# Bias of the first pair straight from the running sums, constants placed behind these, and output tiles copied in halves by two engines

## The chip, the core and the metric

The kernel runs on one core of a Trainium2 chip. The core has five engines with queues of their own: TensorE (PE: matmuls and transposes), VectorE (DVE), ScalarE (ACT), GpSimd (POOL), and SyncE (SP), which issues most of the DMAs; ScalarE issues some. Each engine takes its instructions in a fixed order and waits on semaphores for what others produce. The metric is the device time of one execution in microseconds.

## The reference

Causal attention over 4 batches of 8 heads, 576 positions and 64 columns a head, with a bias from running sums of `s`; the heads side by side are 2304 tokens of 512 columns, and two MLPs of width 2048 follow.

```
scores = q @ k.T / 8
cum    = cumsum(max(s, 0))
scores = where(causal, -1e9, scores + min(-(cum[:, None] - cum[None, :]), 0))
x      = softmax(scores) @ v
h      = relu(x @ w_in);  x = (h * h) @ w_out
h      = x @ w2_in;       out = max(0.01 * h, h) @ w2_out
```

## The kernel before

All matmuls are made from high and low halves of float32 values (three passes, `PASSES`), so each operand is split: ScalarE copies the high half, another engine subtracts it to get the low half.

**Attention** (to about 370 us) goes over 16 pairs of heads; two heads share the 128 partitions. `load_qk` brings q and k (for the first pair alone with `i=0`: k by ScalarE's queue, q by SP's; for the second with `i=1`; then for two pairs at a time). `turn` (L252) transposes k and q on VectorE into a tile of tag `yt`, copies the high half on ScalarE and subtracts on GpSimd. The tag `yt` has two buffers, and so have most others that matter here one to four: a tile that takes a buffer must wait until whoever used it is done. Here `running_sums` (L179) uses both buffers of `yt` first, for `one` and `neg`, and `turn` of the first pair takes them next.

The bias enters the scores as a fourth matmul over four rows a head: `ag` holds, for the queries and the keys, rows of the running sum `ka` (high and low), of ones and of minus ones. `running_sums` clamps `s`, scans it, makes `ka` on VectorE, and writes all four kinds of rows for all heads to the DRAM scratch `aug`; `load_bias` (L246) reads a pair's rows back into `ag`, which GpSimd cleared before.

For each pair, `STEPS` gives seven steps of scores (kinds 0, 2, 3 and 4 for the two heads): `scores` on TensorE, `maxima` on VectorE with the mask (L315), `exponentials` on ScalarE (L339), two steps later `flip` (transposes on TensorE, L349, and copies out), then `values`, `gather`, `spread` and `scale`. Kind 4 is the last 64 rows of both heads at once (L289). Two banks of tag `S` hold scores; the next scores wait until the maxima have read them. Between these, weights are converted one by one by `weight` (L98 to L112): first step on ScalarE (L103, L106) and VectorE (L104, L105), then GpSimd (L108) and VectorE (L109, L111). The staging tile `wst` has one buffer in this stage, so the DMA of a weight goes out when L109 of the one before is done. Matmuls of the first MLP layer (`up1`) fill TensorE's gaps.

**The MLPs** follow: the rest of `up1`, `down1`, and from about 645 us `layer2`, over blocks of 512 tokens (the last of 256). In `layer2` each of 16 chunks `fc` gives hidden values `g`, and `down` adds a chunk to one accumulator bank for each 128 tokens; the last two chunks of a block are added at its end, then ScalarE copies each bank to a tile `o` and SP issues its DMA to the output.

**Order.** A scheduler with a timeline of its own sets the order in which each engine's queue is filled; `after(i)` puts instructions of the same engine as `i` behind `i` and says nothing of other engines. So a change in one place can move instructions elsewhere. DMAs take turns on eight semaphores: a DMA is issued only when the one that used its semaphore before has landed.

## Time and profile before

| | |
|---|---|
| median of 3 runs | 1044.83 us (1044.23 to 1047.97) |
| the profiled execution | 1046.09 us, of it the span 1044.3 us |
| TensorE busy | 1002.3 us, 96% of the span |
| VectorE busy | 558.3 us, 53% |
| ScalarE busy | 519.5 us, 50% |
| GpSimd busy | 226.1 us, 22% |
| chain that ended last | TensorE 56%, DMA 4%, VectorE 2% |

The profile is one execution. An engine's busy share over the whole span says little about a single stage: the same engine can be what all others wait for in one stretch and be free in the next. A row of a timeline gives the start, the duration, the engine, the line and the operation with its tiles (out<-in); a row may hold several instructions that follow each other (xcount), and in brackets stands the idle time of the engine before it and what ended it. PEclk is TensorE's granted clock as a share of the full one.

### The profile page before, as it was taken

How to read it: one execution, taken by the hardware profiler on the slowest of the kernel's cores; microseconds unless marked ns; L12 is line 12 of the kernel's file. 1: busy time of each engine (PE TensorE's matmuls, PEld its weight loads, DVE VectorE, ACT ScalarE, POOL GpSimd, SP SyncE). 2: the span in 40 equal slices, each digit the busy share in tenths (PEclk: the TensorE clock that was granted, in tenths of full speed). 3: DMA queues.
4: the chain of work that ended last, by engine and by line, in shares of the span. 5: the costliest groups of instructions: out<-in, count | busy, mean ns of one | idle time of the engine just before them, and what ended most of it. 6: DMA issues, size and time to landing. Idle time of an engine off the chain costs nothing.

```text
span 1044.3 us, 15068 instructions
## 1 busy us (share of the span) xinstructions
PE 1002.3 (96%) x5312; PEld 834.2 (80%) x5312; DVE 558.3 (53%) x1262; ACT 519.5 (50%) x1126; POOL 226.1 (22%) x294
## 2 busy tenths in 40 slices
PE   4878989899999999999999999999999999999998
PEld 3666867778888878898788889888888888888897
DVE  5778878873586524777875448753222322322322
ACT  4667878886787656754443334533312322322232
POOL 6455546631232002223221112210000000000000
PEclk9999999899999999999999999999999999999999
DMA  7546465453532155866775447401100200100010
GB/s 140 116 119 131 115 181 128 137 117 110 126 93 94 53 173 187 267 192 199 235 227 174 132 143 226 133 24 37 44 1 1 81 1 1 61 1 1 1 41 21
DMA packets 152476, 111.30 MB, mean 107 GB/s; under 512 B 98992, under 2 KB 121008, under 8 KB 152400
## 3 DMA queue, kind: packets, MB, share of 16 engines
q1 hardware_dynamic: 139072, 91.01, 31.6%
q10 hardware_dynamic: 13328, 19.32, 5.2%
q8 instruction: 42, 0.69, 0.3%
q14 instruction: 34, 0.28, 0.1%
HBM read 76.69 MB, written 33.62 MB: 106 GB/s over the span
## 4 chain that ended last, share of the span: by engine, by line
PE 56%; DMA 4%; DVE 2%; issue 1%; ACT 1%; POOL 0%; ACTq 0%; SPq 0%; DVEq 0%; POOLq 0%
PE tr L682 19%; PE h L692 9%; PE S L692 9%; PE h L477 6%; PE tr L657 6%; PE S L657 3%; PE h L657 3%; DMA wst<-in_moe_w_in_dram 2%; DMA wst<-in_moe_w_out_dram 1%; DVE wt L109 1%; DMA gl<-gscr 1%; ACT wt L103 0%; DMA xh<-xscr 0%; DVE gh L442 0%; DMA xscr<-xo 0%
## 5 line engine op out<-in xcount | busy, mean ns | idle before, releaser
L477 PE MATMUL h<-xs,w 128*128 128x512 f32 (+1 forms) x960 | 228.0, 382 | 2.9 <-DVE w L111 1.3
L477 PEld LDWEIGHTS h<-xs,w 128*128 128x128 f32 x960 | 162.7, 191 | 33.0 <-DVE w L111 2.1
L682 PE MATMUL tr<-wo,g 128*128 128x512 f32 x756 | 180.9, 389 | 0.0
L682 PEld LDWEIGHTS tr<-wo,g 128*128 128x128 f32 x756 | 141.1, 188 | 28.8
L108 POOL TENSOR_TENSOR wt<-wt,wst 128x512 uint32<-128x512 uint32 x64 | 90.1, 1408 | 287.7 <-DVE wt L105 232.2
L698 DVE TENSOR_TENSOR r<-S,r 128x512 f32<-128x512 f32 (+1 forms) x40 | 25.5, 637 | 170.1 <-ACT r L697 170.1
L657 PE MATMUL tr<-gh,wo 128*128 128x512 f32 (+1 forms) x576 | 111.9, 354 | 0.0
L692 PE MATMUL S<-xs,w 128*128 128x512 f32 (+1 forms) x480 | 106.9, 368 | 1.1 <-ACT xs L441 1.1
L692 PE MATMUL h<-xs,w 128*128 128x512 f32 (+1 forms) x480 | 107.3, 368 | 0.0
L657 PEld LDWEIGHTS tr<-gh,wo 128*128 128x128 f32 x576 | 94.8, 189 | 14.6
L339 ACT ACTIVATE t<-t,m 128x128 f32<-128x128 f32 (+2 forms) x144 | 83.2, 580 | 35.5 <-DVE m L315 35.0
L692 PEld LDWEIGHTS S<-xs,w 128*128 128x128 f32 x480 | 84.8, 188 | 16.9 <-ACT xs L441 1.6
L692 PEld LDWEIGHTS h<-xs,w 128*128 128x128 f32 x480 | 84.9, 188 | 15.7
L697 ACT ACTIVATE r<-S 128x512 f32<-128x512 f32 (+1 forms) x40 | 22.2, 555 | 147.5 <-PE S L692 147.4
L315 DVE CUSTOM_DVE_ANT_0 t<-S,mask 128x128 f32<-128x128 f32 (+2 forms) x144 | 64.7, 480 | 46.4 <-PE S L299 20.9
L442 DVE TENSOR_TENSOR gh<-gl,gh 128x512 fp32r<-128x512 f32 (+1 forms) x80 | 62.2, 780 | 48.0 <-ACT gh L441 47.5
L441 ACT ACTIVATE gh<-gl 128x512 fp32r<-128x512 f32 (+1 forms) x80 | 46.2, 586 | 76.6 <-PE h L657 36.3
L349 PE MATMUL tr<-ident,t 128*128 128x128 f32 x384 | 69.1, 290 | 10.0 <-ACT t L339 8.8
L442 DVE TENSOR_TENSOR g<-r,g 128x512 fp32r<-128x512 f32 (+1 forms) x80 | 50.9, 644 | 38.5 <-ACT g L441 36.6
L441 ACT ACTIVATE g<-r 128x512 fp32r<-128x512 f32 (+1 forms) x80 | 46.6, 589 | 43.5 <-DVE r L698 43.5
L103 ACT ACTIVATE wt<-wst 128x512 f32<-128x512 f32 x64 | 42.5, 664 | 50.8 <-DMA wst<-in_moe_w_in_dram 35.8
L349 PEld LDWEIGHTS tr<-ident,t 128*128 128x128 f32 x384 | 46.5, 145 | 25.8 <-ACT t L339 13.7
(105 smaller groups left out, 1450.3 us busy)
## 6 DMA issues: line engine op xcount, KB each, us to landing
wst<-in_moe_w_in_dram SPq DMA_DIRECT2D x32, 512.0 KB, 4.0
gscr<-gs ACTq DMA_DIRECT2D x32, 512.0 KB, 4.4
wst<-in_moe_w_out_dram SPq DMA_DIRECT2D x32, 512.0 KB, 3.9
gl<-gscr SPq DMA_DIRECT2D x64, 256.0 KB, 2.8
xscr<-xo SPq DMA_DIRECT2D x32, 144.0 KB, 2.5
out_dram<-o SPq DMA_DIRECT2D x18, 256.0 KB, 2.4
xh<-xscr SPq DMA_DIRECT2D x16, 256.0 KB, 2.8
zscr<-ys SPq DMA_DIRECT2D x16, 256.0 KB, 3.5
```

What stands on the lines that cost most here:

```text
L103: nc.scalar.activation(f32(t), f32(hw), AF.Abs)
L108: nc.gpsimd.tensor_tensor(t, t, lw, ALU.add)
L315: return nc.vector.tensor_tensor_reduce(t[:, a:z], sc, msk, -QK_SCALE, first, ALU.add, ALU.min, m).ins
L339: done = nc.scalar.activation(t[:, a:z], t[:, a:z], AF.Exp, bias=m[:, c:c + 1], scale=-1.0, accum_out=sums[:, s0:s0 + 1])
L349: nc.tensor.transpose(tr[:, c * P:(c + 1) * P], t[:, c * P:(c + 1) * P], ident)
L441: a = nc.scalar.activation(out[0], x, AF.Copy)
L442: b = nc.vector.tensor_tensor(out[1], x, f32(out[0]), ALU.subtract)
L477: nc.tensor.matmul(h[:, :w], win[0, fc][:, a, c * P:(c + 1) * P], xs[j, c][:, z, :w], start=(c == 0 and y == 0), stop=(c == KC - 1 and y = ...
L657: nc.tensor.matmul(y[e][:, :w], wout[0, fc][:, a, e * P:(e + 1) * P], gh[:, z, :w], start=(fc == 0 and x == 0), stop=(fc == FC - 1 and x = ...
L682: nc.tensor.matmul(acc[i], g[:, a, i * P:(i + 1) * P], wout[1, fc][:, z], start=(fc == 0 and x == 0), stop=(fc == FC - 1 and x == 2))
L692: nc.tensor.matmul(h[:, :w], win[1, fc][:, a, c * P:(c + 1) * P], xs[c][:, z, :w], start=(c == 0 and x == 0), stop=(c == KC - 1 and x == 2))
L698: nc.vector.tensor_tensor(r[:, :w], h[:, :w], r[:, :w], ALU.max)
```

## The change

Four things are changed.

1. **First pair's bias.** `running_sums` gets the first pair's `ag` and issues six small DMAs into it straight from `ka` and `neg` (four of one row for both heads, by SP and ScalarE in turn, and two from `neg`). The constant rows of `ag` (ones on the query side, zeros on the key side) are written by ScalarE beforehand. The four DMAs to `aug` are issued behind these, all by SP; `load_bias` does nothing for the first pair.
2. **Constants and memsets.** The memsets of `ident`, `mask` and `mask4` are written together ahead of the loads, and GpSimd's selects and memsets stand under `after(raw["sums"])`, the scan.
3. **First pair's low halves** of q and k are subtracted by VectorE, no longer by GpSimd.
4. **End of a block in `layer2`.** `down` is written tile by tile, and each tile `o` is copied in two halves of 256 columns, by ScalarE and VectorE, and sent by two DMAs, by SP and ScalarE.

```diff
@@ -167,16 +167,13 @@
             before[i.engine] = i
 
     def constants():
-        nc.vector.memset(ident, 0.0)
         nc.gpsimd.affine_select(ident, ident, [[-1, P]], ALU.not_equal, 1.0, 0, 1)
-        nc.vector.memset(mask, 0.0)
         nc.gpsimd.affine_select(mask[:, S - P:], mask[:, S - P:], [[-1, P]], ALU.is_ge, -1.0e9 / QK_SCALE, 0, 1)
-        nc.vector.memset(mask4, 0.0)
         for p0 in (0, 64):
             nc.gpsimd.affine_select(mask4[p0:p0 + 64, S // 2 - 64:], mask4[p0:p0 + 64, S // 2 - 64:], [[-1, 64]],
                                     ALU.is_ge, -1.0e9 / QK_SCALE, 0, 1)
 
-    def running_sums(at):
+    def running_sums(at, ag):
 
         sp, cum = [at.tile([BH, S], F32, tag="t", name="t", bufs=TB) for _ in range(2)]
         one, neg = [at.tile([BH, S], F32, tag="yt", name="yt", bufs=2) for _ in range(2)]
@@ -186,13 +183,21 @@
         nc.gpsimd.memset(neg, -1.0)
         yield
         nc.vector.tensor_scalar(sp, sp, 0.0, 1.0 / QK_SCALE, ALU.max, ALU.mult)
-        nc.vector.tensor_tensor_scan(cum, one, sp, 0.0, ALU.mult, ALU.add)
+        raw["sums"] = nc.vector.tensor_tensor_scan(cum, one, sp, 0.0, ALU.mult, ALU.add).ins
         nc.vector.tensor_copy(ka[:, 0], cum)
         nc.vector.tensor_tensor(ka[:, 1], cum, f32(ka[:, 0]), ALU.subtract)
-        nc.sync.dma_start(aug[:, 0:2, 0], one.unsqueeze(1).to_broadcast([BH, 2, S]))
-        nc.sync.dma_start(aug[:, 2:4, 1], neg.unsqueeze(1).to_broadcast([BH, 2, S]))
-        nc.sync.dma_start(aug[:, 0:2, 1], f32(ka))
-        nc.scalar.dma_start(aug[:, 2:4, 0], f32(ka))
+        h0, h1 = pairs[0].h
+        for z in range(2):
+            nc.sync.dma_start(f32(ag[z:z + 65:64, 1]), f32(ka[h0:h1 + 1:h1 - h0, z]))
+            nc.scalar.dma_start(f32(ag[2 + z:z + 67:64, 0]), f32(ka[h0:h1 + 1:h1 - h0, z]))
+        for e in range(2):
+            raw["sent"] = nc.sync.dma_start(f32(ag[64 * e + 2:64 * e + 4, 1]), neg[0:2]).ins
+        yield
+        with after(raw["sent"]):
+            nc.sync.dma_start(aug[:, 0:2, 1], f32(ka))
+            nc.sync.dma_start(aug[:, 2:4, 0], f32(ka))
+            nc.sync.dma_start(aug[:, 0:2, 0], one.unsqueeze(1).to_broadcast([BH, 2, S]))
+            nc.sync.dma_start(aug[:, 2:4, 1], neg.unsqueeze(1).to_broadcast([BH, 2, S]))
 
     class Pair:
 
@@ -246,6 +251,8 @@
     def load_bias(x):
         p = pairs[x]
         p.ag, p.last = ags[x % 2]
+        if x == 0:
+            return
         for e in range(2):
             nc.sync.dma_start(f32(p.ag[64 * e:64 * e + 4]), aug[p.b * H + p.h[e]])
 
@@ -259,7 +266,7 @@
         yt = at.tile([P, S], F32, tag="yt", name="yt", bufs=2)
         nc.vector.transpose(yt, raw[which][:, p.i])
         nc.scalar.activation(hi, yt, AF.Copy)
-        nc.gpsimd.tensor_tensor(lo, yt, f32(hi), ALU.subtract)
+        (nc.vector if x == 0 else nc.gpsimd).tensor_tensor(lo, yt, f32(hi), ALU.subtract)
 
     def turn_v(at, x, e):
         p = pairs[x]
@@ -497,24 +504,30 @@
         for x in range(2):
             ags.append((at.tile([P, 2, S], F32R, tag=f"ag{x}", name=f"ag{x}"),
                         at.tile([P, 3, P], F32R, tag=f"la{x}", name=f"last{x}")))
-        sums = running_sums(at)
+        warm = at.tile([P, 64], F32, tag="warm", name="warm")[:, 0:1]
+        for t in (warm, ident, mask, mask4):
+            nc.vector.memset(t, 0.0)
+        sums = running_sums(at, ags[0][0])
         next(sums)
         load_qk(at, 0, 0)
-        warm = at.tile([P, 64], F32, tag="warm", name="warm")[:, 0:1]
-        nc.vector.memset(warm, 0.0)
         with after(raw["issued"]):
             nc.scalar.activation(warm, warm, AF.Exp)
-        constants()
-        for t in ags[0]:
-            nc.gpsimd.memset(f32(t), 0.0)
-        next(sums, None)
+        nothing = warm.to_broadcast([P, S])
+        for z in range(2):
+            nc.scalar.activation(ags[0][0][:, z], nothing, AF.Copy, scale=0.0, bias=1.0 - z)
+        next(sums)
+        with after(raw["sums"]):
+            constants()
         turn(at, 0, "k")
         turn(at, 0, "q")
+        next(sums, None)
         load_bias(0)
         load_qk(at, 0, 1)
         load_v(at, 0)
-        for t in ags[1]:
-            nc.gpsimd.memset(f32(t), 0.0)
+        with after(raw["sums"]):
+            nc.gpsimd.memset(f32(ags[1][0]), 0.0)
+            for x in range(2):
+                nc.gpsimd.memset(f32(ags[x][1]), 0.0)
         scores(0, 0)
 
         for x in range(len(pairs)):
@@ -676,8 +689,8 @@
             xs.append(t)
         acc = [bank("tr") for _ in range(w // P)]
 
-        def down(fc, g):
-            for i in range(w // P):
+        def down(i, *chunks):
+            for fc, g in chunks:
                 for x, (a, z) in enumerate(PASSES):
                     nc.tensor.matmul(acc[i], g[:, a, i * P:(i + 1) * P], wout[1, fc][:, z],
                                      start=(fc == 0 and x == 0), stop=(fc == FC - 1 and x == 2))
@@ -700,13 +713,17 @@
             tick(*done)
             prev.append((fc, g))
             if len(prev) > DEPTH:
-                down(*prev.pop(0))
-        for x in prev:
-            down(*x)
+                chunk = prev.pop(0)
+                for i in range(w // P):
+                    down(i, chunk)
         for i in range(w // P):
+            down(i, *prev)
             o = lo.tile([P, DM], F32, tag="yf", name="o", bufs=OB)
-            nc.scalar.activation(o, acc[i], AF.Copy)
-            nc.sync.dma_start(out[n + i * P:n + (i + 1) * P, :], o)
+            rows, half = slice(n + i * P, n + (i + 1) * P), DM // 2
+            nc.scalar.activation(o[:, :half], acc[i][:, :half], AF.Copy)
+            nc.vector.tensor_copy(o[:, half:], acc[i][:, half:])
+            nc.sync.dma_start(out[rows, :half], o[:, :half])
+            nc.scalar.dma_start(out[rows, half:], o[:, half:])
 
     late = ctx.enter_context(ExitStack())
     with tc.tile_pool(name="mg", bufs=1) as mg, tc.tile_pool(name="mx", bufs=1) as mx:
```

How instructions stand in the queues, at three places. First SyncE's queue from the start of the program on (`t` is `s`, `yt` is `one` or `neg`), before:

```order
L184 DMA t<-in_s_dram 32x576
L226 DMA qr<-in_q_dram 32x18x32 x4
L192 DMA aug<-yt 32x2x576
L193 DMA aug<-yt 32x2x576
L194 DMA aug<-ka 32x2x576
L226 DMA kr<-in_k_dram 32x18x32 x3
L250 DMA ag_83<-aug 4x1152 x2
L226 DMA kr<-in_k_dram 32x18x32
```

and with the change:

```order
L181 DMA t<-in_s_dram 32x576
L231 DMA qr<-in_q_dram 32x18x32 x4
L231 DMA kr<-in_k_dram 32x18x32 x3
L191 DMA ag_83<-ka 2x576 x2
L194 DMA ag_83<-yt 2x576 x2
L197 DMA aug<-ka 32x2x576
L198 DMA aug<-ka 32x2x576
L199 DMA aug<-yt 32x2x576
L200 DMA aug<-yt 32x2x576
L231 DMA kr<-in_k_dram 32x18x32
```

The reads of `one` and `neg` (`aug<-yt`) have moved from ahead of the sums to behind them and behind six other DMAs, and three loads of k for the second pair have moved ahead of the sums.

Second, GpSimd's queue at the start, with what each instruction waits for, before:

```order
L186 MEMSET yt 32x576
L171 ISA
L171 AFFINE_SELECT ident<-ident 128x128 [waits DVE_49]
L509 MEMSET ag_83 128x1152
L509 MEMSET last_84 128x384
L241 MEMSET vp 64x128
L517 MEMSET ag_85 128x1152
L517 MEMSET last_86 128x384
```

and with the change:

```order
L183 MEMSET yt 32x576
L170 ISA
L170 AFFINE_SELECT ident<-ident 128x128 [waits DVE_49]
L246 MEMSET vp 64x128
L528 MEMSET ag_85 128x1152
L530 MEMSET last_84 128x384
L530 MEMSET last_86 128x384
L246 MEMSET vr 64x128
```

One of the two long memsets is gone; the others wait for nothing, as before, and the select waits for VectorE's count, which the memset of `ident` raises.

Third, ScalarE's queue at the end of the third pair and the start of the fourth (L339 and L346 are the exponentials, L103 and L106 the first step of a weight, L593 and L606, L400 and L407 copies out of TensorE's banks), before:

```order
L400 ACTIVATE xo<-tr 64x320 x2
L593 ACTIVATE pT_686<-tr 128x3x128
L339 ACTIVATE t,sums<-t,m 128x512
L103 ACTIVATE wt<-wst 128x512
L106 ACTIVATE wst<-wst 128x512
L400 ACTIVATE xo<-tr 64x256
L339 ACTIVATE t,sums<-t,m 128x512
L400 ACTIVATE xo<-tr 64x256
L593 ACTIVATE pT_686<-tr 128x4x128
L339 ACTIVATE t,sums<-t,m 128x576
L339 ACTIVATE t,sums<-t,m 128x128
L339 ACTIVATE t,sums<-t,m 128x256
```

and with the change:

```order
L407 ACTIVATE xo<-tr 64x320 x2
L103 ACTIVATE wt<-wst 128x512
L106 ACTIVATE wst<-wst 128x512
L346 ACTIVATE t,sums<-t,m 128x512
L606 ACTIVATE pT_691<-tr 128x3x128
L407 ACTIVATE xo<-tr 64x256
L346 ACTIVATE t,sums<-t,m 128x512
L407 ACTIVATE xo<-tr 64x256
L606 ACTIVATE pT_691<-tr 128x4x128
L346 ACTIVATE t,sums<-t,m 128x576
L346 ACTIVATE t,sums<-t,m 128x128
L103 ACTIVATE wt<-wst 128x512
```

Both weights' first steps have moved up, the one ahead of an exponential of 512 columns, the other (before, three exponentials further down) ahead of the last three exponentials of a step; on VectorE, L104 has moved up likewise, ahead of a copy and a maximum, and on TensorE the eight matmuls of the last rows (L289) have moved behind four transposes and two matmuls of the values.

## Rows read from the trace of the kernel before

**Rows 1.** Busy time by stretch: stretch, length, busy time of each engine (instructions), PEclk, DMA.

```profile
660.00:1040.00 380.00, 380.00 (x1767) 318.14 (x1765) 123.36 (x204) 110.97 (x199) 8.84 (x6) 1.00 0.08 26
```

**Rows 2.** Timeline of VectorE at the start: start, duration, engine, line, operation.

```profile
2.90 2.07 DVE L188 TENSOR_SCALAR t<-t 32x576 f32<-32x576 f32 x1 [1.40 <-DMA t<-in_s_dram]
5.07 1.35 DVE L189 TENSOR_TENSOR_SCAN t<-yt,t 32x576 f32<-32x576 f32 x1
6.45 0.45 DVE L190 CAST ka<-t 32x576 fp32r<-32x576 f32 x1
6.94 0.75 DVE L191 TENSOR_TENSOR ka<-t,ka 32x576 fp32r<-32x576 f32 x1
7.61 0.76 DVE L260 STREAM_TRANSPOSE yt<-kr 128x576 f32<-128x576 f32 x1
```

**Rows 3.** Timeline of GpSimd at the start.

```profile
2.10 1.05 POOL L509 MEMSET ag<- 128x1152 f32 x1
...
4.60 0.72 POOL L517 MEMSET last<- 128x384 f32 x1
...
9.24 2.75 POOL L262 TENSOR_TENSOR Y<-yt,Y 128x576 fp32r<-128x576 f32 x2 [1.45 <-ACT Y L261]
```

**Rows 4.** Timeline of all engines up to the first scores.

```profile
8.40 1.34 ACT L261 ACTIVATE Y<-yt 128x576 fp32r<-128x576 f32 x2 [4.07 <-DVE yt L260]
...
10.60 0.62 SPq L250 DMA_DIRECT2D ag<-aug  x2
...
12.05 0.69 PE L299 MATMUL S<-Y 64*128 64x128 f32 x4 [1.77 <-POOL Y L262]
...
12.71 0.81 PE L299 MATMUL S<-ag 64*128 64x128 f32 x2
```

**Rows 5.** DMA issues from 0 to 20 us: queue, count, size, us to landing.

```profile
aug<-ka SPq DMA_DIRECT2D x1, 144.0 KB, 2.1
```

**Rows 6.** Timelines of ScalarE, VectorE and TensorE at the third and fourth pairs.

```profile
53.62 0.72 ACT L339 ACTIVATE t<-t,m 128x512 f32<-128x512 f32 x1
55.77 0.66 ACT L103 ACTIVATE wt<-wst 128x512 f32<-128x512 f32 x1 [1.35 <-DMA wst<-in_moe_w_in_dram]
57.16 0.71 ACT L339 ACTIVATE t<-t,m 128x512 f32<-128x512 f32 x1
63.77 0.68 ACT L103 ACTIVATE wt<-wst 128x512 f32<-128x512 f32 x1 [0.95 <-DMA wst<-in_moe_w_in_dram]
64.92 1.24 ACT L261 ACTIVATE Y<-yt 128x576 fp32r<-128x576 f32 x2
56.47 0.43 DVE L104 TENSOR_SCALAR wt<-wt 128x512 f32<-128x512 f32 x1 [2.01 <-ACT wt L103]
59.32 0.68 DVE L109 SCALAR_TENSOR_TENSOR wt<-wst,wt 128x512 uint32<-128x512 uint32 x1
53.80 0.66 PE L289 MATMUL S<-Y,last 128*128 128x288 f32 x3
58.01 0.66 PE L349 MATMUL tr<-ident,t 128*128 128x128 f32 x4 [1.79 <-ACT t L339]
58.81 0.55 PE L299 MATMUL S<-Y 64*128 64x128 f32 x6
73.94 0.84 PE L289 MATMUL S<-Y,last 128*128 128x288 f32 x3 [2.68 <-DVE m L315]
```

**Rows 7.** Busy time by stretch, as in group 1.

```profile
72.00:76.00 4.00, 2.06 (x10) 2.05 (x11) 2.90 (x9) 1.78 (x5) 2.80 (x6) 0.78 0.52 153
```

**Rows 8.** Timelines of ScalarE and SyncE at the end.

```profile
1036.10 0.38 ACT L697 ACTIVATE r<-h 128x256 f32<-128x256 f32 x1 [1.14 <-PE h L692]
1039.98 1.09 ACT L708 ACTIVATE o<-tr 128x512 f32<-128x512 f32 x2 [2.59 <-PE tr L682]
1040.60 0.82 SPq L709 DMA_DIRECT2D out_dram<-o  x2
```

**Rows 9.** VectorE's instructions by line and shape: count, busy us, mean ns.

```profile
L662 DVE COPY ys<-tr 128x256 f32<-128x256 f32 x2 | 0.8, 408 | 0.0
```

## The prediction

> **What bounds the kernel now.** I read the busy table by stretches first. From 660 to 1040 us TensorE is busy without a gap [rows 1], so nothing that happens beside it there can move the time, and the change leaves TensorE's order there alone. Time can be won or lost only before the first scores, in the attention stage while TensorE still waits for other engines, and after the last matmul.
>
> Next I read the start engine by engine. VectorE's clamp of `s` begins when `s` has landed, at 2.90, and takes 2.07 us, while a cast of the same 576 columns takes 0.45; the reader is to see GpSimd's long memsets over the same microseconds [rows 2, 3]. Scan, cast, subtraction and the transposes follow each other without a gap [rows 2]. ScalarE makes the high halves, GpSimd the low ones (2.75 for both), and TensorE's third matmul starts at 12.05, released by GpSimd; the bias, which went out to DRAM and came back, is there at 12.71 [rows 3, 4]. So two chains end within 0.7 us: the low halves on GpSimd, and the bias by way of `aug`. To gain, the change has to shorten both.
>
> Then the third and fourth head pairs (44 to 80 us), because the order of the changed kernel differs there. ScalarE converts a weight tile in its first step (L103) when its DMA has landed, and waits for that at 55.77 and at 63.77; VectorE's L104 waits for L103 at 56.47; TensorE stands 1.79 us at 58.01 and 2.68 us at 73.94 [rows 6]. Whatever stands behind L103 or L104 on its engine waits for the weight too.
>
> Last, the end: two copies from 1039.98 on and two DMA issues from 1040.60 [rows 8].
>
> **The change part by part.** *Memsets and constants.* The masks' memsets on VectorE move a line, to the same place: nothing. The `after(raw["sums"])` names an instruction of VectorE, and what stands under it runs on GpSimd; in the order of the changed kernel GpSimd's selects wait for the memsets only and its memsets for nothing, so they are not behind the sums in time. What does change is that `ag` of the first pair (1.05 us) leaves GpSimd for ScalarE, which is idle then. From 2.1 on GpSimd still has one memset of 1152 columns (1.05), two of 384 (a third of that each) and two small ones of some 0.2: to about 4.15. The clamp starts at 2.90 again. Before, it ended at 4.97, that is, it got through when the second long memset ended near 4.6, and the `last` memset that started there took 0.72 [rows 2, 3]. If it gets through at the end of the one long memset that is left (3.3), it ends at 3.75; if only after the last memset, at 4.6. I take the middle, 4.2: 0.8 us gained, with 0.4 to 1.2 as ends.
>
> The Trainium skill (SBUF — State Buffer, section Who interferes with whom) calls the port pair that VectorE and GpSimd share an exclusive lock, held for one whole instruction. By that the clamp would follow the memset that is running and end at 3.75, and the sum would be 0.45 us lower; the row of before speaks against it, since there GpSimd began three more memsets while the clamp waited [rows 2, 3].
>
> *Bias without the round trip.* From 4.2: scan 1.35, cast 0.45, subtraction 0.75 and gaps of 0.05 give the cast at 6.1 and the subtraction at 6.9 [rows 2]. The six small DMAs into `ag` go out between 6.1 and 7.8 on SP and ScalarE and land 2.1 us after their issue (the landing of `aug<-ka`) [rows 5], at 9.9 at the latest. So the bias no longer ends last.
>
> *A new wait.* `one` and `neg` are the two buffers of tag `yt`, and the transposes of k and q write into these two. Before, their DMAs to `aug` were issued at about 4 us and were done when the transposes came. Now the same two DMAs (L199, L200) stand last of eight on SP, behind the sums. SP needs 0.31 us an issue [rows 4]: first `ag` at 6.1, second 6.9, the two from `neg` 7.2 and 7.5, L197 7.85. L198 takes a semaphore that ScalarE's first `ag` DMA (6.1) has to give back, so it goes at 8.3; L199 at 8.6; L200, behind ScalarE's second one, at 9.05. They land 2.1 later: 10.7 and 11.2. Queued behind the waiting transposes on VectorE are the two subtractions that were GpSimd's; behind those, ScalarE's and TensorE's first work. k's transpose 10.7 to 11.5, q's to 12.25 (0.76 each [rows 2]), the high half of q to 12.95 (half of 1.34 [rows 4]), the low half on VectorE, priced as the subtraction of as many columns at 0.75, to 13.75. TensorE's third matmul starts at 13.8 and not at 12.05: **+1.7 us**. The ends: clamp early, 1.3; clamp late, 2.1; landings 0.3 shorter or 0.7 longer. Taking 2.75 us off GpSimd earns nothing, since the transposes are late. The three k loads that now stand ahead on SP are issued by 5.3 and hide under the sums.
>
> *The order at the third and fourth pairs.* On ScalarE L103 and L106 now stand ahead of the first 512-column exponential of the third pair, and L104 on VectorE ahead of a copy and the second maximum. (Times as before; the 1.7 comes on top.) The weight still lands at 55.75, since its DMA is issued behind the same loads. So the exponential that ran at 53.62 runs at 57.1, after L103 and L106 of 0.66 each; L104 ends at 56.9, copy and second maximum at 58.1, the second exponential starts at 58.5 instead of 57.16 [rows 6]. TensorE, with the transposes of the first exponential ahead, stands from 53.9 to 57.75, then does 0.5 of transposes, 0.8 of values once the copies have freed its bank (58.9), and the eight matmuls of the last rows, which the order has put behind these (1.2 [rows 6]), to 60.8. Two maxima of 0.5 with L109 (0.7) between them end at 61.9, and the next pair's scores start at 62.0 and not at 58.81: 3.2 late. L109 ends at 61.45, before at 60.0, so the next weight lands 1.45 later, at 65.2. There L103 and L106 have been moved ahead of three exponentials (1.5 us in all): the high half of k, at 64.92 before, comes at 67.9 [rows 6], GpSimd's low half, its weight step, L109, and the matmul of 73.94 with them. **+3.0 us**; ends 0 (the weight is there in time) and 5.
>
> *Last tiles.* TensorE's last rows are in the same order in both kernels, so the first tile is not done earlier. VectorE's half copy waits for ScalarE's half of the same tile, not for TensorE alone. From 1039.98: ScalarE's halves of 0.38 to 1040.36 and 1040.75, VectorE's of 0.41 to 1040.8 and 1041.2 [rows 8, 9]. The last issue is at 1041.2, before at 1041.1, but it carries 128 KB behind 384 KB that went earlier: **-0.2 us**, ends -0.4 and +0.2. At the four block ends before, copies and issues lie under matmuls [rows 1]: nothing.
>
> The Trainium skill (Trainium Kernel Development and Optimization, section Key Constraints) says that DMAs from all queues run on the same 16 engines and that a second queue saves issue time only; by that the tail gains no transfer time, which would put the sum at its upper end, +0.2. No row here has two queues at once at the end.
>
> The sum: +1.7 + 3.0 - 0.2 = **+4.5 us**. The profiled execution took 1046.09 us (span 1044.3), so it would be 1050.6; that execution lies 1.3 above the median of the runs, and for the median 1044.83 I forecast **1049.3**.
>
> **The rivals.** *Only the start is late.* If the weights land before ScalarE comes to them, the moved L103 costs nothing: 1044.83 + 1.7 - 0.2 = 1046.3. Against it: ScalarE waited for both of these weights [rows 6]. *The start is faster, as written.* If the transposes find their buffers free, they run from 6.95, the low half is done at 9.9 and TensorE is 2.1 us early; with the order costing nothing, 1042.5. Against it: two buffers, and a read of each that is issued after the sums. *Slower, by the clock.* The stretch of 3.85 us in which TensorE stands at the third pair may lower its granted clock. Before, after a stand of 2.68 us, the granted clock was 0.78 from 72 to 76 [rows 7], and three matmuls that had taken 0.66 took 0.84 [rows 6]; TensorE then has 3.0 us of work on the chain, which takes 0.8 more at that ratio and 3.0 more at the lower of the two levels; I take 1.5, and 1.0 for the fourth pair: 1049.3 + 2.5 = 1051.8. It decides once the new stand ends with the clock lowered while TensorE has the chain. Against it: the stand of 1.79 at 58.01 lowered nothing, and the drop of 72 to 76 may be gone then.
>
> **How the numbers follow.** Half a per cent, about what a measurement of this kernel can tell from no change, ends at 1050.05 and 1039.6. Forecast 0.42, of which 0.11 lies above 1050.05 by the upper ends of its terms; late start alone 0.22; fast start 0.10, of which 0.02 below 1039.6; clock 0.26, 0.24 of it above. Slower 0.35, faster 0.02, within 0.63. The range from 1043.5 to 1052.5 leaves out most of the fast start and the upper part of the clock case, near 0.2; the forecast's own is 1046.5 to 1051.
>
> **What would show it.** The clamp's duration (0.9 to 1.7 if right). k's transpose starting after 10, released by a DMA. TensorE's third matmul at 13 to 14.5. L103 of the second weight idle ahead of the first 512-column exponential, and the next pair's scores 4 to 5 us later than 58.81. Granted clock between 58 and 64. The last DMA issued near 1041.2 plus the delay. I am wrong if the transposes start before 8, if the third pair is no later than the first, or if the delay shrinks between 80 and 200 us, where TensorE still has gaps.

## The result, and the profile after

| | before | changed |
|---|---|---|
| median, measured together | 1045.76 us | 1053.78 us |
| ratio (95% interval) | | 1.0080 (1.0063 to 1.0097) |
| the profiled execution | 1046.09 us, span 1044.3 | 1053.75 us, span 1051.9 |

The change makes the kernel 8.0 us slower on the medians (7.7 between the profiled executions). The forecast was 4.5 slower, and 1053.8 lies above the range, which ended at 1052.5: the direction was right, the size and the upper end were wrong. Of the 4.5 us by which 1053.8 lies above the forecast of 1049.3, 0.9 is the kernel before itself, which took 1045.76 beside the changed one and not 1044.83.

In the changed kernel's listing lines lie elsewhere. At the start: clamp L185, subtraction L188, the transposes L267, high halves L268, low halves L269; the small DMAs to `ag` L191, L192 and L194, those to `aug` L197 to L200. Then: scores L306, last rows L296, maxima L322, exponentials L346, `flip` L356, values L396. L103 to L112 stayed.

The start on VectorE (start, duration, engine, line, operation, and the idle time before it with what ended it), against [rows 2]:

```profile
2.85 1.48 DVE L185 TENSOR_SCALAR t<-t 32x576 f32<-32x576 f32 x1 [1.34 <-DMA t<-in_s_dram]
...
6.30 0.75 DVE L188 TENSOR_TENSOR ka<-t,ka 32x576 fp32r<-32x576 f32 x1
12.73 0.78 DVE L267 STREAM_TRANSPOSE yt<-kr 128x576 f32<-128x576 f32 x1 [5.69 <-DMA aug<-yt]
13.49 0.78 DVE L267 STREAM_TRANSPOSE yt<-qr 128x576 f32<-128x576 f32 x1
14.26 1.52 DVE L269 TENSOR_TENSOR Y<-yt,Y 128x576 fp32r<-128x576 f32 x2
```

The sums are ready at 7.05, 0.65 us earlier than before, and then VectorE stands 5.69 us for the DMA that reads `one`. SyncE's issues over the same time, and TensorE's first scores, against [rows 4]:

```profile
6.34 1.33 SPq L191 DMA_DIRECT2D ag<-ka  x2
7.77 1.21 SPq L194 DMA_DIRECT2D ag<-yt  x2
9.03 0.39 SPq L197 DMA_DIRECT2D aug<-ka  x1
9.47 0.42 SPq L198 DMA_DIRECT2D aug<-ka  x1
9.94 0.43 SPq L199 DMA_DIRECT2D aug<-yt  x1
```

```profile
15.83 0.69 PE L306 MATMUL S<-Y 64*128 64x128 f32 x4 [0.32 <-DVE Y L269]
16.32 0.42 PE L306 MATMUL S<-ag 64*128 64x128 f32 x2
```

The third matmul comes at 15.83 (12.05 before). The bias does follow without a wait, as the change meant, so the first maximum starts 3.2 us late (17.85 for 14.64) and not 3.8. The third pair, ScalarE, SyncE and TensorE, against [rows 6], and the busy time by stretch there (length, PE, PEld, DVE, ACT, POOL, then PEclk, DMA share, GB/s):

```profile
59.91 0.66 ACT L103 ACTIVATE wt<-wst 128x512 f32<-128x512 f32 x1 [4.98 <-DMA wst<-in_moe_w_in_dram]
...
61.02 0.72 ACT L346 ACTIVATE t<-t,m 128x512 f32<-128x512 f32 x1
```

SyncE's four loads of q ahead of that weight's DMA, before and with the change:

```profile
47.45 3.15 SPq L222 DMA_DIRECT2D qr<-in_q_dram  x4
```

```profile
51.00 4.01 SPq L227 DMA_DIRECT2D qr<-in_q_dram  x4
```

TensorE:

```profile
61.89 1.11 PE L356 MATMUL tr<-ident,t 128*128 128x128 f32 x4 [4.51 <-ACT t L346]
62.79 1.49 PE L396 MATMUL tr<-pT,vp 128*128 128x256 f32 x4
63.93 1.07 PE L296 MATMUL S<-Y,last 128*128 128x288 f32 x3
...
67.80 0.55 PE L306 MATMUL S<-Y 64*128 64x128 f32 x6 [0.32 <-DVE m L322]
```

```profile
60.00:64.00 4.00, 2.11 (x9) 1.94 (x9) 3.29 (x9) 3.29 (x8) 0.60 (x1) 0.57 0.07 16
64.00:68.00 4.00, 3.68 (x20) 3.26 (x18) 1.76 (x7) 1.14 (x3) 0.69 (x1) 0.58 0.30 69
```

The reader sees ScalarE stand 4.98 us for the weight with the exponential behind it, TensorE 4.51 us for that exponential, and then the work that the next scores wait for at 0.57 of the clock (the mean over the stretch of its two levels, 1.00 and 0.50): three matmuls of the last rows take 1.07 where they took 0.66. The end:

```profile
1047.77 0.66 ACT L723 ACTIVATE o<-tr 128x256 f32<-128x256 f32 x2 [2.59 <-PE tr L695]
1048.18 0.81 SPq L725 DMA_DIRECT2D out_dram<-o  x2
1048.64 0.89 ACTq L726 DMA_DIRECT2D out_dram<-o  x2
```

From the first copy to the end of the span are 4.13 us, before 4.32 [rows 8].

So the delay grows like this. First scores of each pair in the profiled executions, in us; the last column tells how long TensorE took for the first six 512-column matmuls of the first pair (0.97 is full speed; 1.65 is half, as e10 took with the granted clock at 0.50; on this more below). Each row is one execution, for e3 and e7 the fastest of its kernel, for e5, e8 and e9 the slowest.

| kernel | 2nd pair | 3rd | 4th | 5th | 6th | 12th | span | six matmuls |
|---|---|---|---|---|---|---|---|---|
| before | 25.47 | 40.64 | 58.81 | 78.55 | 99.32 | 242.33 | 1044.3 | 0.97 |
| changed | 28.77 | 43.93 | 67.80 | 85.77 | 108.16 | 251.01 | 1051.9 | 0.96 |
| e1 | 26.46 | 41.63 | 60.37 | 79.99 | 101.14 | 244.33 | 1046.7 | 1.65 |
| e2 | 25.26 | 40.42 | 64.04 | 81.93 | 103.61 | 246.81 | 1048.8 | 1.03 |
| e3 | 31.38 | 46.26 | 64.80 | 84.39 | 105.03 | 247.12 | 1047.8 | 1.65 |
| e4 | 24.66 | 39.98 | 59.11 | 77.34 | 99.33 | 244.24 | 1044.8 | 0.96 |
| e5 | 30.40 | 45.57 | 64.92 | 82.90 | 104.84 | 247.91 | 1049.6 | 1.65 |
| e6 | 28.44 | 43.61 | 66.42 | 84.58 | 106.21 | 248.48 | 1050.3 | 0.97 |
| e7 | 24.61 | 39.78 | 58.99 | 77.26 | 98.94 | 241.87 | 1043.0 | 1.65 |
| e8 | 27.43 | 42.60 | 60.94 | 80.69 | 102.29 | 244.67 | 1046.8 | 1.65 |
| e9 | 24.48 | 43.34 | 61.77 | 80.54 | 101.88 | 247.38 | 1048.8 | 0.96 |
| e10 | 23.41 | 41.99 | 60.63 | 79.16 | 101.22 | 244.02 | 1047.0 | 1.65 |
| e11 | 29.67 | 44.84 | 67.05 | 85.22 | 108.18 | 251.97 | 1053.1 | 1.65 |
| e12 | 30.08 | 45.25 | 66.02 | 84.07 | 107.08 | 249.97 | 1051.1 | 1.65 |

Changed against before: +3.3 at the second pair, 5.7 more over the third, and of these 9.0 some 1.2 are given back by the last matmul (7.8), 0.2 at the end. The fourth pair gives 1.8 back and the fifth takes 1.6 again; there the granted clock falls (in e6, where it stays at 1.00, this pair takes 0.8 less):

```profile
88.00:92.00 4.00, 2.41 (x15) 1.55 (x16) 3.48 (x13) 2.64 (x11) 2.08 (x4) 0.91 0.00 0
92.00:96.00 4.00, 3.52 (x8) 2.14 (x8) 3.59 (x12) 2.66 (x7) 3.53 (x5) 0.50 0.97 188
```

### The profile page after: what moved, and what is told of

Its sections match the earlier page's. It is cut to its first block, busy times and chain, and to the rows that moved or that the text cites. A ratio compares the mean times of both kernels' runs of the same rounds, so it can differ in the third digit from the quotient of the medians.

```text
span 1051.9 us, 15123 instructions
## 1 busy us (share of the span) xinstructions
PE 1003.2 (95%) x5312; PEld 834.9 (79%) x5312; DVE 566.1 (54%) x1282; ACT 517.4 (49%) x1128; POOL 224.7 (21%) x291
## 4 chain that ended last, share of the span: by engine, by line
PE 79%; DMA 6%; DVE 6%; ACT 3%; POOL 2%; issue 2%; SPq 1%; DVEq 0%; ACTq 0%; POOLq 0%
PE tr L695 19%; PE h L484 15%; PE h L705 9%; PE S L705 9%; PE tr L670 8%; PE S L670 4%; PE h L670 4%; DMA wst<-in_moe_w_in_dram 4%; PE tr L396 4%; PE tr L356 3%; PE S L306 2%; PE S L296 1%; DVE t L322 1%; ACT t L346 1%; DVE wt L109 1%
## 5 line engine op out<-in xcount | busy, mean ns | idle before, releaser
L346 ACT ACTIVATE t<-t,m 128x128 f32<-128x128 f32 (+2 forms) x144 | 83.4, 581 | 33.9 <-DVE m L322 32.9
L322 DVE CUSTOM_DVE_ANT_0 t<-S,mask 128x128 f32<-128x128 f32 (+2 forms) x144 | 64.8, 481 | 44.8 <-PE S L306 19.3
L356 PE MATMUL tr<-ident,t 128*128 128x128 f32 x384 | 69.5, 292 | 17.1 <-ACT t L346 14.7
L356 PEld LDWEIGHTS tr<-ident,t 128*128 128x128 f32 x384 | 46.9, 146 | 33.2 <-ACT t L346 19.7
L103 ACT ACTIVATE wt<-wst 128x512 f32<-128x512 f32 x64 | 42.5, 664 | 55.0 <-DMA wst<-in_moe_w_in_dram 38.2
```

The source lines that it names most:

```text
L103: nc.scalar.activation(f32(t), f32(hw), AF.Abs)
L322: return nc.vector.tensor_tensor_reduce(t[:, a:z], sc, msk, -QK_SCALE, first, ALU.add, ALU.min, m).ins
L346: done = nc.scalar.activation(t[:, a:z], t[:, a:z], AF.Exp, bias=m[:, c:c + 1], scale=-1.0, accum_out=sums[:, s0:s0 + 1])
L356: nc.tensor.transpose(tr[:, c * P:(c + 1) * P], t[:, c * P:(c + 1) * P], ident)
```

## The experiments

Each ratio is to the kernel before, measured beside the run. Differences between two versions are taken from their ratios, by which the changed kernel is 8.4 us slower (8.0 on the medians); with the intervals such a difference is uncertain by 2 to 3 us.

**e1, buffers of their own for `one` and `neg`.**

```diff
-        one, neg = [at.tile([BH, S], F32, tag="yt", name="yt", bufs=2) for _ in range(2)]
+        both = at.tile([BH, 2, S], F32R, tag="pT1", name="both", bufs=2)
+        one, neg = f32(both[:, 0]), f32(both[:, 1])
```

> The changed kernel, but `one` and `neg` lie in one tile of tag `pT1`, so the first transposes find the buffers of `yt` free; the queues of TensorE, and those of ScalarE and VectorE at the third and fourth pairs, come out as in the kernel before. Theory (late start plus moved queues make the whole loss): k's transpose near 7.1, the third matmul of the first scores at 10 to 12 (bias landing last), the third and fourth pairs paced as before, so about 1 us faster than the kernel before (1 to 2 less span). Rival 1 (the loss sits in the rest of the change: six small DMAs, ScalarE's rows of `ag`, tiles in halves): still 3 us or more slower than before. Rival 2 (the start alone makes the loss, by way of later loads): same time as the theory says, so this run does not part the two; the next does.

Measured: 1.0006 (0.9994 to 1.0018) of before, so all but 0.6 of the 8.4 us are gone with the wait and the moved queues; but the 1 us gain did not come. The third matmul came at 10.29, 1.8 us early. VectorE's transpose of the second pair's q then waited for its load, with a maximum behind it, and in this execution TensorE was at half speed until 24 us:

```profile
10.29 0.69 PE L307 MATMUL S<-Y 64*128 64x128 f32 x4 [0.46 <-DVE Y L270]
```

```profile
15.98 0.78 DVE L268 STREAM_TRANSPOSE yt<-qr 128x576 f32<-128x576 f32 x1 [1.26 <-DMA qr<-in_q_dram]
```

The rest of the change (small DMAs, ScalarE's rows of `ag`, halves), together with the earlier start, costs nothing that can be measured. A cost of the rest that the earlier start pays for is not ruled out.

**e2, e1 with the low halves on GpSimd.**

```diff
-        (nc.vector if x == 0 else nc.gpsimd).tensor_tensor(lo, yt, f32(hi), ALU.subtract)
+        nc.gpsimd.tensor_tensor(lo, yt, f32(hi), ALU.subtract)
```

> As e1, and the low halves of the first pair subtracted by GpSimd again. By this the queues of TensorE and ScalarE come out exactly as in the changed kernel, moved weight steps and all, while the transposes do not wait. Theory: the start is about as before (third matmul 12 to 14, within 2 us of before), but ScalarE waits for the second weight ahead of the 512-column exponential and TensorE stands over 3 us at the third pair: 4 to 6 us lost there, so 4 to 7 us slower than the kernel before and 5 or more slower than e1. Rival (the start alone): within 2 us of the kernel before.

Measured: 1.0051 (1.0033 to 1.0069), 5.3 us slower than before, as the theory said, and 4.7 slower than e1. The start is on time (25.26), yet ScalarE and TensorE:

```profile
56.16 0.66 ACT L103 ACTIVATE wt<-wst 128x512 f32<-128x512 f32 x1 [4.99 <-DMA wst<-in_moe_w_in_dram]
```

```profile
58.13 1.12 PE L357 MATMUL tr<-ident,t 128*128 128x128 f32 x4 [4.51 <-ACT t L347]
...
64.04 0.55 PE L307 MATMUL S<-Y 64*128 64x128 f32 x6 [0.32 <-DVE m L323]
```

Without any late start the third pair loses 5.4 us: the moved queues are a cause by themselves. No single part of the change moves them: at these pairs e1, e3 and e4 have the order of the kernel before, e2 that of the changed kernel.

**e3, the changed kernel with the low halves on GpSimd** (the diff of e2 alone).

> The changed kernel with the low halves of the first pair on GpSimd; the transposes still wait for the reads of `one` and `neg`, but the queues at the third and fourth pairs come out as in the kernel before. Theory: late start alone, third matmul near 17, first scores 3 to 5 us late, and no stand of TensorE of over 2.5 us at the third pair: 3 to 4.5 us slower than the kernel before, and faster than the changed kernel by 3 to 5. Rival (the start alone makes the loss of the changed kernel): as slow as the changed kernel or slower, 8 us over the kernel before.

Measured: 1.0049 (1.0025 to 1.0073), 5.1 us slower than before (more than the 3 to 4.5 expected) and 3.2 faster than the changed kernel. Third matmul at 17.34, 1.5 behind the changed kernel with the low halves on GpSimd, second pair 5.9 late (some of it the half speed of the start), and the third pair takes 18.54 us from its first scores to the next pair's, before 18.17. Late, but in the old order: TensorE stands 2.17 us there (before 1.79) and not 4.51.

**e4, reads of `one` and `neg` for `aug` ahead of the sums** (L199 and L200 moved ahead of the small DMAs).

> The changed kernel with the two reads of `one` and `neg` for `aug` issued where the kernel before issued them, ahead of the sums. The small DMAs from `neg` into `ag` are still issued behind the sums, so k's transpose is free at 7.1 but q's waits for these. Queues at the third and fourth pairs as in the kernel before. Theory: q's transpose at 10.5 to 12, third matmul at 12.5 to 14, 0 to 2 us slower than the kernel before; 2 us slower than e1. Rival (the late DMA reads are not what holds the transposes): start as late as in the changed kernel, third matmul near 15.8.

Measured: 1.0005 (0.9993 to 1.0016). k's transpose ran at 6.97, q's at 9.56 and not at 10.5 to 12, the third matmul at 11.90:

```profile
6.97 0.76 DVE L267 STREAM_TRANSPOSE yt<-kr 128x576 f32<-128x576 f32 x1
...
8.76 0.76 DVE L269 TENSOR_TENSOR Y<-yt,Y 128x576 fp32r<-128x576 f32 x1 [1.03 <-ACT Y L268]
9.56 0.78 DVE L267 STREAM_TRANSPOSE yt<-qr 128x576 f32<-128x576 f32 x1
```

So the late reads held the transposes until 12.73. With the reads early, k's does not wait, and q's follows k's low half, which this version's order puts ahead of it; the small DMAs from `neg` do not hold it beyond that. The time is that of e1 and not 2 us above it.

**e5, the changed kernel's instructions in e1's order.** At the end of the program a few lines chain every engine's instructions in a recorded order, by dependences that set the order of the queue and no wait.

```diff
+            for a, z in zip(row, row[1:]):
+                tc.add_manual_dep(z, a.name, mybir.DependencyInfo(
+                    mybir.DependencyClass.NoSync, mybir.DependencyReason.DATA), reason="queue")
```

> The changed kernel with no instruction altered, but every engine's queue held, for the whole program, in the order that the queues have in e1 (at the third and fourth pairs the order of the kernel before). It differs from e1 only by the wait for `one` and `neg`, and from the changed kernel only by the order. Theory: third matmul at 15.8 as in the changed kernel, first scores of the second to fourth pairs at 28.8, 43.9 and 62 (before: 25.47, 40.64, 58.81), no stand of TensorE over 2.5 us at the third pair, 3 to 3.5 us slower than the kernel before and 4 to 5 faster than the changed kernel. Rival (the lateness of the start makes the weight late, whatever the order): fourth pair at 66 to 68, as slow as the changed kernel.

Measured: 1.0038 (1.0025 to 1.0051), 4.0 us slower than before, and 4.4 faster than the changed kernel. TensorE at the third pair:

```profile
64.12 0.66 PE L399 MATMUL tr<-ident,t 128*128 128x128 f32 x4 [1.05 <-ACT t L389]
...
64.92 0.55 PE L349 MATMUL S<-Y 64*128 64x128 f32 x6
```

The fourth pair is later than expected (64.92 for 62) because this execution's start ran at half speed (30.40 for 28.8) and the third pair took 1.2 us more than before, with the granted clock at 0.62 from 52 to 56, where it was 1.00 before. With e1, which differs by the wait alone, the late start costs 3.3 us (1.0038 less 1.0006), and the moved queues on top of it 4.4 (1.0080 less 1.0038).

**e6, TensorE kept busy in its stand.** Queues held in the changed kernel's order.

```diff
+                    idle = bank("h")
+                    raw["idle"] += [nc.tensor.transpose(idle[:, :P], ident, ident).ins for _ in range(36)]
                 jobs = flip(at, zx, *STEPS[zs], live.pop(z))
```

> The changed kernel with all queues held in its own order, and 36 transposes of `ident` into an idle bank put into TensorE's queue where it stands 4.51 us at the third pair (36 of 0.11 us are 4 us, so they end before the stand does). Theory: of the 5.7 us that the third pair loses, about 2 are the lowered clock after the stand (0.57 of full speed from 60 to 68): with TensorE busy the granted clock stays at 1.00 there, the fourth pair's first scores come at 65.5 to 66.3 and not at 67.80, and the whole is 1 to 2.5 us faster than the changed kernel. Rival (the wait alone, the clock costs nothing on the chain): 67.5 to 68, and the time of the changed kernel.

Measured: 1.0054 (1.0037 to 1.0071), 2.7 us less than the changed kernel, just clear of the noise.

```profile
58.57 4.09 PE L647 MATMUL h<-ident 128*128 128x128 f32 x36
62.50 0.60 PE L399 MATMUL tr<-ident,t 128*128 128x128 f32 x4
...
66.42 0.55 PE L349 MATMUL S<-Y 64*128 64x128 f32 x6 [0.94 <-DVE m L365]
```

```profile
60.00:64.00 4.00, 4.00 (x37) 3.95 (x36) 3.23 (x9) 2.85 (x8) 1.26 (x1) 1.00 0.22 53
64.00:68.00 4.00, 3.06 (x33) 2.68 (x32) 2.78 (x12) 1.64 (x4) 0.98 (x4) 1.00 0.45 122
```

From the first transpose behind the stand to the fourth pair's scores are 3.92 us; in the changed kernel and in e2 5.91. The lowered clock is worth 2.0 us there. (The transposes ended 1.3 us after the exponential was done, so a part of the gain was not had: the fourth pair came at 66.42, 37.98 us behind the second pair's scores for 39.03, and not at 65.5 to 66.3.)

**e7, e1 with the second pair's loads ahead of the DMAs to `aug`.**

```diff
-        next(sums, None)
         load_bias(0)
         load_qk(at, 0, 1)
+        next(sums, None)
```

> e1 with the last five loads of k and q for the second pair issued ahead of the four DMAs to `aug` and not behind them; all other queues as in e1. In e1 the third matmul came 1.8 us earlier than before, yet the second pair's first scores came 1.0 us later, at 26.46. Theory: VectorE's transpose of the second pair's q, which waited for its load until 15.98, holds the maxima behind it and lets TensorE stand; with the load 1.8 us earlier the second pair's scores come at 24 to 25.2, and the time is 1 to 2 us below e1 and about 1 below the kernel before. Rival (TensorE's low clock up to 24 us makes it, whatever the loads do): 26 to 26.5, and the time of e1.

Measured: 1.0014 (0.9999 to 1.0028). The profiled execution (1044.78, the median is 1048.09) does what the theory says: second pair at 24.61, 1.9 before e1 with the same half-speed start. The median is not faster. Why its other executions are slower than this one no trace shows; that stays open.

**e8, the tiles in halves alone** (the last hunk of the change on the kernel before).

> The kernel before with the last part of the change alone (tiles copied in halves, sent by two queues). All of attention as before. Theory: 0.2 us less from the first copy of the last block to the end of the span (4.1 for 4.3), and nothing at the other block ends: no difference in the time beyond 0.3 us. Rival (halves on VectorE, or DMA issues on ScalarE, hold up the chunks that follow a block end): 1 us slower or more, with idle time of TensorE at 700 to 950 us.

Measured: 1.0001 (0.9990 to 1.0011), TensorE without a gap from 660 us on, 4.28 us from the first copy to the end. The start, which is that of the kernel before, showed what was not expected. The same six matmuls, before and in e8:

```profile
19.76 0.97 PE L299 MATMUL S<-Y 64*128 64x512 f32 x6
```

```profile
19.78 1.65 PE L299 MATMUL S<-Y 64*128 64x512 f32 x6
```

**e9, the kernel before with TensorE busy from 2 us on.**

```diff
+        t = bank("h")
+        for _ in range(40):
+            nc.tensor.transpose(t[:, :P], ident, ident)
         scores(0, 0)
```

> The kernel before, all queues held in its own order, with 40 transposes of `ident` into an idle bank at the head of TensorE's queue, where it stands until 9.8 us. In the kernel before and in e8, whose starts are the same to 0.05 us, the first six 512-column matmuls took 0.97 us in one run and 1.65 in the other, and the second pair's first scores came at 25.47 and 27.43. Theory (TensorE starts at half speed and comes to full speed at a moment that differs by some 4 us from run to run, which is the difference between the two): with TensorE busy from 2 us on, the first scores already run at full speed, the six matmuls take 0.97, and the second pair's scores come at 23 to 25; 1 to 2 us faster than the kernel before on the median. Rival (something else in the start, a load or another engine, differs between runs): still 25.5 or 27.4 and no change of the time.

Measured: 0.9996 (0.9983 to 1.0010). Half right: the first scores did run at full speed (the first two matmuls, at 9.80, took 0.33 for 0.48, the six 0.96) and the second pair came at 24.48. In the profiled execution the granted clock then fell, and by the third pair's first scores (43.34 for 40.64) more than the gain was gone:

```profile
12.00:16.00 4.00, 2.68 (x19) 2.06 (x21) 1.98 (x10) 1.70 (x8) 1.66 (x8) 0.84 0.78 140
16.00:20.00 4.00, 3.85 (x23) 2.40 (x22) 3.06 (x9) 3.25 (x9) 1.78 (x4) 0.73 0.58 134
32.00:36.00 4.00, 4.00 (x14) 3.11 (x13) 0.99 (x4) 2.22 (x6) 1.38 (x4) 0.60 0.48 127
```

With TensorE busy from the start the executions still lie between 1044.66 and 1050.62, no closer together than those of the kernel before measured beside them (1045.16 to 1049.96). So, if all of them start at full speed as the profiled one did, the moment of full speed is not what mainly sets the executions apart.

**e10, e7 with 34 such transposes at the head, and 19 and 14 in the stands of the fourth and fifth pairs.**

> e7 (buffers of their own, loads ahead of the DMAs to `aug`) with all queues held, 34 transposes of `ident` at the head of TensorE's queue, and 19 and 14 of them where TensorE stands 2.8 and 2.3 us ahead of the last rows of the fourth and fifth pairs. Theory: the direct bias is worth its 1.8 us once the transposes do not wait and TensorE is at full speed from the first scores: second pair's scores at 22 to 23 (before 25.47 or 27.43), granted clock at 1.00 up to 150 us, and 3 to 5 us faster than the kernel before. Rival (the early start is lost again at the loads or weights behind it, as in e1 and e7): within 1 us of the kernel before, or of e9 if that is faster.

Measured: 1.0020 (1.0003 to 1.0036). 2.1 us slower than before: the theory fails, and the rival holds in so far as the early start is lost, though more than its 1 us. Second pair at 23.41, 2.1 early, third at 41.99, 1.4 late, with the granted clock at 0.50 to 0.68 from 12 to 20 and at 0.76 to 0.82 from 28 to 36. No version here beats the kernel before.

**e11, e6 with 24 transposes.**

> e6 with 24 transposes in place of 36. In e6 the weight came 0.7 us earlier than in the changed kernel and the 36 transposes ended 1.3 us after the exponential that they were to bridge. Measured from the first scores of the second pair to those of the fourth: before 33.34, e5 34.52, changed 39.03, e6 37.98 us. Theory (2.0 us of the third pair's loss are the lowered clock, 3.7 the wait for the weight): granted clock 1.00 after the stand, 36.7 to 37.3 us. Rival (the clock falls again, since TensorE still stands some 2 us): 38.5 to 39.

Measured: 1.0070 (1.0045 to 1.0095). 37.38 us (the theory nearly: 36.7 to 37.3) from the second pair's scores to the fourth's, and again 4.10 behind the stand at full clock (62.95 to 67.05). But the whole is hardly faster than the changed kernel (1.0 us, within the noise). The clock now fell in the fourth pair:

```profile
64.00:68.00 4.00, 3.06 (x33) 2.81 (x31) 3.21 (x10) 2.23 (x6) 1.74 (x3) 1.00 0.52 125
68.00:72.00 4.00, 2.89 (x19) 1.84 (x16) 3.97 (x17) 1.85 (x5) 1.67 (x3) 0.68 0.62 220
72.00:76.00 4.00, 3.60 (x8) 2.50 (x9) 3.06 (x8) 4.00 (x14) 2.12 (x2) 0.50 0.02 4
```

Yet that pair took 18.17 us, 0.2 more than in the changed kernel, where the clock was full: the lower clock took the place of a stand of 1.78 us ahead of the last rows. In the profiled executions the 1.65 us won up to the fourth pair are more than lost to a start 0.9 later, 0.6 at the fifth pair and 0.9 between the sixth and the twelfth; for the last two no cause is shown.

**e12, the second weight's DMA ahead of the last two loads of q** in SyncE's queue, all else in the changed kernel's order.

```diff
 DMA qr<-in_q_dram 32x36x32 x2
+DMA wst<-in_moe_w_in_dram 128x4x256
 DMA qr<-in_q_dram 32x36x32 x2
-DMA wst<-in_moe_w_in_dram 128x4x256
```

> The changed kernel, all queues held in its own order except SyncE's, where the DMA of the second weight goes ahead of the last two of the eight loads of k and q that it stood behind. The weight's buffer is free at 53.4 and the DMA was issued at 55.12, landing at 59.91. Theory (ScalarE waits for this DMA and nothing else): issued at 53.5, ScalarE's step at 58.2 to 58.6, TensorE's stand 2.8 to 3.2 and not 4.51; from the second pair's first scores to the fourth's 37 to 37.6 us if the clock still falls, 35.2 to 35.8 if not (changed 39.03); the time 1.5 to 3.5 us below the changed kernel's. Rival (the transfers share what there is, so the weight lands no earlier; or another wait holds ScalarE): 38.5 or more.

Measured: 1.0056 (1.0035 to 1.0077), 2.5 us below the changed kernel, which the noise of both does not let be sure; the stretch shows more.

```profile
59.96 0.66 ACT L146 ACTIVATE wt<-wst 128x512 f32<-128x512 f32 x1 [2.02 <-DMA wst<-in_moe_w_in_dram]
```

This start was 1.3 us later than the changed kernel's (half speed), so counted from the second pair's scores ScalarE's step came at 29.9 and not 31.1. The stand was 1.55 us and not the 2.8 to 3.2 of the theory: 1.3 less by the earlier weight, and 1.7 less because TensorE itself came to it that much later, with the granted clock at 0.67 from 52 to 56. Behind the stand the clock was at its full level, and second to fourth pair took 35.94, not 39.03. ScalarE waits for this DMA, and its place behind the loads sets when it lands. In the fourth pair the clock then fell:

```profile
64.00:68.00 4.00, 2.96 (x31) 2.35 (x29) 3.22 (x15) 1.82 (x5) 2.17 (x4) 1.00 0.73 197
68.00:72.00 4.00, 2.76 (x12) 2.03 (x13) 3.47 (x13) 2.66 (x11) 0.71 (x2) 0.53 0.38 138
72.00:76.00 4.00, 4.00 (x14) 2.80 (x14) 2.57 (x6) 3.26 (x10) 3.22 (x4) 0.61 0.00 0
```

## Why the prediction was right in direction and too small

Three steps of the sum failed, all too low: the price of an issue on SP, 0.31 us, which measured 0.57 to 0.64 for these DMAs; the weight's landing, taken "as before", which came 0.85 later; and the clock behind the stand, which the forecast put at nothing and left to a rival, and which cost 2.0.

- **Clamp, 0.8 us earlier: right.** It ended at 4.33 (4.2 predicted), 0.64 earlier than before, and took 1.48 (0.9 to 1.7). By the Trainium skill (SBUF — State Buffer, section Who interferes with whom) whoever issues first gets the shared pair for the whole instruction. By that VectorE would have got through behind the long memset, at 3.75, if the clamp alone takes the 0.45 of the cast. The trace does not agree: 4.33, after GpSimd had begun three more memsets.
- **Bias no longer last: right.** Its matmul follows at once (16.32).
- **The new wait, +1.7: right mechanism, wrong size.** It cost 3.3 us (second pair's scores; e5 against e1). The term that failed is "SP needs 0.31 us an issue". The row behind it, two issues of 0.62 [rows 4], was for other DMAs. The four small ones on SP took 0.57 to 0.64 each, those to `aug` about 0.4, so L199 went at 9.94 and not at 8.6: 1.3 us, 0.1 of it from the sums. The landing took 2.8 from the issue instead of 2.1: 0.7 more, inside the bounds that I gave. So the third matmul came at 15.83 and not at 13.8; 0.5 of that came back because the bias no longer follows later than the low halves. My bounds had no place for the price of an issue, though no row showed one for such a DMA.
- **Order at the third pair, +3.0: right mechanism, wrong size.** Measured 5.7 in the changed kernel, 5.4 in e2 with a start on time. The stand was 4.51 and not 3.85, and 2.0 us came from the clock. The step "the weight still lands at 55.75" failed: apart from the start, it landed 0.6 later in e2 and 0.85 in the changed kernel, where the four loads of q ahead of its DMA took 4.01 to issue, 3.15 before (e12 shows that its place behind these loads sets the landing; why they took longer stays open).
- **The fourth pair, no more than carried on: right over two pairs, not for each.** It gave 1.8 back: the fall of the clock from 72 to 76 [rows 7] was gone, which the rival had held possible, and from the last rows' first matmul to the next pair's scores TensorE took 3.0 us (82.76 to 85.77), before 4.6 (73.94 to 78.55). The fifth took 1.6 again; both together took 40.36 us, before 40.51. The delay did not shrink between 80 and 200 us as a whole (7.2 at the fifth pair, 8.8 at the sixth, 8.7 at the twelfth).
- **The rival by the clock: true at the third pair, and priced well there** (1.5, measured 2.0); its 1.0 for the fourth pair did not come. Its mistake was where it stood: as a case that excluded the forecast's own upper bounds. The errors all pointed upward: 1.6 at the start, 0.7 at the weight, 2.0 of clock; the start's stands apart from the others (e2), while the clock's comes with the stand (e6). The forecast's 4.5 and these are 8.8, of which 1.2 were given back by the end; what gave them back no run separates. A range over cases that add up has to reach to the sum of their upper ends.
- **Tail, -0.2: not shown.** It took 4.13 for 4.32 here, but 4.28 in e8 with the same copies, and it is too small to be seen in the time.
- **Rivals that fell:** only the start late (e2), a start faster as written (12.73), the rest of the change (e1).

## What to carry to other kernels

A buffer is free when the last transfer that reads it has landed: when a transfer is moved behind a computation, look for whoever takes its source next. A change at the start of a scheduled program can move the queues a long way behind it, and a step that waits for a DMA must not be put ahead of work that TensorE is waiting for; here that cost 4.4 us, the late transposes 3.3. An early gain need not last: the 1.8 us that e1 had at the third matmul were gone by the second pair, and the 2.1 that e10 had there by the third.

## What the runs showed of the hardware

- TensorE started at half speed, the lower of its two levels, when it had not worked before (its first two matmuls took 0.48 us, in e9 behind 40 transposes 0.33), and the moment when it came to full speed differed between executions with the same queues: by 19.8 us in the kernel before, after 24.5 in e8, with the scores ahead of that within 0.13 us of each other. It is worth 2.0 us at the second pair (25.47 and 27.43). The column of the granted clock shows 1.00 in both from 0 to 28 us, so at the start the durations must be read instead.
- Where added transposes kept TensorE busy the granted clock stayed at 1.00 (e6 from 60 to 68, in the changed kernel 0.57), but in e9, e10 and e11 it fell in later stretches (0.60 from 32 to 36, 0.50 from 16 to 20, 0.50 from 72 to 76), so full speed won at one stage was not won for the whole. It also fell in runs without added transposes (e5, e12). What decides where it falls, these runs do not show.
- A DMA of two rows of 576 values from one SBUF tile to another took SyncE 0.57 to 0.64 us to issue, one of 32x2x576 to DRAM 0.39 to 0.43 in the changed kernel and 0.30 to 0.37 before: the price of an issue is not fixed by its shape alone.
